# Output products moved inside the rounds of half-size products, one more at a chunk's head, no round in the chunk of the last values, and another buffer in the tail

## The chip, the cores and the metric

One core of one Trainium2 chip. The metric is the device time of one execution in microseconds (us). The kernel before takes 332.12 us (median of 3 runs, 332.07 to 332.22). "Span" is what the profiler sees of an execution, from its first to its last instruction or transfer; the time was 1.7 to 3.6 us longer than the span in these runs.

## The reference, cut to what matters

Pooled attention, then a gated two-layer block. Batch 8, 8 heads, 576 rows, head size 64; 4608 tokens of 512 values, inner size 1536.

```python
def _attn_ref(q, k, v):                      # k and v are averaged over 8 rows first
    scores = scale * np.matmul(q, k_p.transpose(0, 1, 3, 2))
    attn = np.exp(scores - scores.max(-1, keepdims=True))
    return np.matmul(attn / attn.sum(-1, keepdims=True), v_p)

def _moe_ref(x, w_gate, w_val, w_out):
    return (np.maximum(x @ w_gate, 0.0) * (x @ w_val)) @ w_out
```

## The kernel before

The tokens are taken in nine chunks of 512 (0 to 8). In each chunk TensorE makes twelve **units** (`gate_val`: eight matmuls of 512 columns, giving one block of 128 rows of `h`), and beside them the output products of the chunk before and the attention of the batch that a later chunk needs. Attention ends in chunk 6: its scores and **values** are woven between the units there, and VectorE has the values to scale.

From chunk 1 on, the output layer uses a scheme with seven half-size products for eight (Strassen's, in Winograd's form). From the end of chunk 6 on, the first layer does so too: a **hidden product** makes two blocks of `h` (fo and fo + 6), which would take two units, with seven half-size products (pr1 to pr7, four matmuls of 256 columns each: 28 in place of the 32 that two units come to). Two of them, x and y, are interleaved into a **round**, with sums of x quarters or of `h` on VectorE between (`s`), and two output products P (twelve matmuls of 256 columns). A **bank** is the tile in TensorE's accumulation memory that a product is written to; before another product may overwrite it, ScalarE has to copy it out or VectorE to add it to something (a **take**).

```python
def hidden_products(c, fo, z):
    ...
    def pr1():
        bank("a")
        product("a", plain(0, fs), e, True)
        nc.scalar.copy(p1, ps["a"])            # ScalarE empties bank a for pr6
    def pr2():
        bank("b", ps_at, "at")
        product("b", plain(1, fs), g, True)
        take("b", p1, fo, lo)()                # take: VectorE adds, GpSimd finishes h
    def pr5():
        bank("c")
        product("c", summed(0), T[0], True)
        nc.scalar.copy(p5, ps["c"])            # ... bank c for pr3
    def pr6():
        product("a", summed(1), T[1], False)
        nc.scalar.copy(u2, ps["a"])            # ... bank a for pr7
    def pr3():
        product("c", summed(3), h, False)
    def pr7():
        product("a", summed(2), T[2], False)
        ends.append(take("a", p5, n_hf + fo, hi, nc.scalar))   # VectorE empties bank a for pr4
    def later():                               # x[9], y[9]
        ends.append(take("c", u2, fo, hi, nc.scalar))
    def pr4():
        product("a", plain(1, fu), T[3], False)
        ...                                    # relu on ScalarE, product on VectorE

def hidden_round(c, fo, others, sums):
    x, y = [hidden_products(c, fo + z, z) for z in range(2)]
    first, second = others
    s = sums
    return [x[1], s[0], x[2], s[1], y[1], y[2], s[2], x[5], s[3], x[6], *first,
            y[5], x[3], x[7], x[9], y[6], y[3], x[4], x[8], y[7], *second, y[9], y[4], y[8]]

def out_products(c, last=False):               # one accumulation bank for all seven
    rows = [half_pool.tile([P, 2, DM], F32, name=f"rows{i}", bufs=2 - i) for i in range(2)]
    ...
    order = [pr1, pr2, pr6, pr7, pr5, pr3, pr4] if last else \
        [pr1, pr2, pr6, pr7, pr4, pr5, pr3]
```

In the text below, "x4" is pr4 of x. Chunk 6 ran eight units and one round, chunk 7 three rounds, chunk 8 two rounds and four units, then a tail that makes chunk 8's own output.

The softmax here doesn't subtract the row's maximum and nothing guards it: scores larger than these inputs give would overflow.

## Time and profile before

| | before |
|---|---|
| time | 332.12 us |
| span of the profiled run | 330.3 us |
| TensorE busy | 96% of the span |
| VectorE busy | 68% |
| rounds of half-size products | 6 (chunk 6 one, chunk 7 three, chunk 8 two) |
| gaps in TensorE's matmul stream from 220 us on, of more than 0.1 us | 9, together 3.86 us |

A matmul's row shows a duration of 0.27 us for 256 columns, but these overlap, so the distance between starts is what counts. A gap is the start of a group less the start of the group before and that group's matmuls times 0.109 us (256 columns) or 0.216 (512). Nine gaps: six before x4 (2.27 us), two before an output product that follows another (1.02), one in the tail (0.57).

### The profile page before, as it was taken

To read this page: it belongs to the slowest core of one execution; us is meant where nothing else is said; L and a number is where in the kernel's file an instruction comes from. 1 tells how busy PE (TensorE), PEld (TensorE's weight loads), DVE (VectorE), ACT (ScalarE), POOL (GpSimd) and SP (SyncE) were. 2 spreads that over 40 slices of the span, in tenths; PEclk is the share of its full clock that TensorE was granted. 3 is DMA by queue.
4 is the path that set the end of the run, shared out by engine and by line. 5 is a ranking of instruction groups with operands and counts; after the bars stand their busy time and mean duration, and the time that the engine had idled before them with its cause. 6 is when DMAs were issued, how large, how long until landed. Compare 5 with 4: busy or idle time off the path is not lost.

```text
span 330.3 us, 7017 instructions
## 1 busy us (share of the span) xinstructions
PE 318.4 (96%) x2670; PEld 226.7 (69%) x2670; DVE 225.7 (68%) x482; ACT 152.1 (46%) x353; POOL 207.0 (63%) x258
## 2 busy tenths in 40 slices
PE   7899999999999999999999999999999999999994
PEld 2577885555566656666989866656668888888673
DVE  7455637667675856696569544974699988878761
ACT  1444482374555227522762266126715665565230
POOL 8557608999999924963399029999604676567100
PEclk9999999999999999999999999999999999999998
DMA  7999998997859439999893480332021310120134
GB/s 110 187 202 202 200 214 146 192 166 143 166 101 176 90 90 107 55 168 179 127 186 65 101 122 0 51 73 82 0 42 33 87 41 2 33 98 3 25 108 123
DMA packets 51011, 35.46 MB, mean 107 GB/s; under 512 B 30433, under 2 KB 45025, under 8 KB 50977
## 3 DMA queue, kind: packets, MB, share of 16 engines
q0 software_dynamic: 18304, 18.88, 36.4%
q1 hardware_dynamic: 32528, 16.00, 26.1%
q8 instruction: 21, 0.34, 0.4%
q10 hardware_dynamic: 144, 0.13, 0.1%
q14 instruction: 14, 0.11, 0.1%
HBM read 37.75 MB, written 9.44 MB: 143 GB/s over the span
## 4 chain that ended last, share of the span: by engine, by line
PE 81%; DVE 11%; DMA 4%; issue 1%; POOL 1%; SPq 1%; ACT 0%; DVEq 0%; POOLq 0%
PE mm_ps L430 42%; PE acc_ps L523 17%; PE mm_ps L743 6%; PE at_ps L311 4%; PE mm_ps L468 3%; PE at_ps L389 3%; DVE sum L514 3%; DVE px L759 2%; DMA out_dram<-rows 2%; DMA q<-in_q_dram 2%; PE at_ps L743 1%; DVE px L395 1%; DVE rows L531 1%; DVE h L439 1%; DVE sum L594 1%
## 5 line engine op out<-in xcount | busy, mean ns | idle before, releaser
L439 DVE TENSOR_TENSOR h<-mm_ps,relu 128x512 f16<-128x512 f32 (+1 forms) x96 | 59.8, 624 | 69.5 <-PE mm_ps L430 60.1
L436 ACT ACTIVATE relu<-mm_ps 128x512 f16<-128x512 f32 (+1 forms) x96 | 52.2, 544 | 101.8 <-PE mm_ps L430 96.4
L430 PE MATMUL mm_ps<-x_T,wg_sb 128*128 128x512 f16 (+1 forms) x432 | 88.5, 331 | 0.0
L430 PE MATMUL mm_ps<-x_T,wv_sb 128*128 128x512 f16 (+1 forms) x432 | 88.4, 332 | 0.0
L430 PEld LDWEIGHTS <-wv_sb 128*128 128x128 f16 x432 | 42.2, 98 | 30.5 <-DVE kpT0u L264 0.2
L430 PEld LDWEIGHTS <-wg_sb 128*128 128x128 f16 x432 | 38.9, 98 | 19.5
L325 ACT ACTIVATE expT<-at_ps 72x288 f16<-72x288 f32 (+2 forms) x128 | 38.9, 375 | 13.7 <-PE at_ps L311 13.6
L523 PEld LDWEIGHTS <-sum 128*128 128x128 f16 x336 | 32.0, 98 | 7.0 <-issue 1.3
L395 DVE TENSOR_TENSOR px<-at_ps,prd 128x256 f16<-128x256 f32 (+1 forms) x80 | 33.8, 423 | 2.7
L181 POOL TENSOR_TENSOR tree_b<-tree_a 72x256 f32<-72x256 f32 (+1 forms) x42 | 33.5, 799 | 3.3
L765 POOL TENSOR_TENSOR h<-px 128x256 f16<-128x256 f16 x36 | 25.4, 718 | 13.7 <-ACT px L762 12.7
L523 PE MATMUL acc_ps<-wo_sums,sum 128*128 128x256 f16 x252 | 30.9, 272 | 0.3 <-DVE mid L531 0.3
L175 POOL TENSOR_TENSOR tree_a<-k_in 96x512 f32<-96x512 f16 x18 | 21.5, 1197 | 14.4 <-DMA k_in<-in_k_dram 14.4
L175 POOL TENSOR_TENSOR tree_a<-v_in 72x512 f32<-72x512 f16 x24 | 28.7, 1197 | 0.1
L523 PEld LDWEIGHTS <-h 128*128 128x128 f16 x252 | 23.7, 98 | 2.8
L764 POOL TENSOR_SCALAR px<-px 128x256 f16<-128x256 f16 x12 | 13.1, 1092 | 18.9 <-DVE px L759 18.9
L843 POOL COPY gate<-h 128x1 f16<-128x1 f16 x4 | 1.5, 381 | 33.7 <-DVE h L439 33.7
L523 PE MATMUL acc_ps<-wo_sb,h 128*128 128x256 f16 x168 | 20.6, 272 | 0.0
L514 DVE TENSOR_TENSOR sum<-h 128x768 f16<-128x768 f16 x28 | 18.8, 670 | 0.0
L531 DVE TENSOR_TENSOR rows<-acc_ps,mid 128x512 f32<-128x512 f32 x21 | 14.4, 686 | 4.9 <-PE acc_ps L523 4.8
L389 PEld LDWEIGHTS <-expT 72*128 72x128 f16 (+1 forms) x280 | 12.9, 100 | 5.9 <-DVE prd L394 0.8
L394 DVE RECIPROCAL prd<-at_ps 128x4 f32<-128x4 f32 (+1 forms) x80 | 13.7, 171 | 3.7 <-PE at_ps L389 3.6
(144 smaller groups left out, 526.0 us busy)
## 6 DMA issues: line engine op xcount, KB each, us to landing
out_dram<-rows SPq DMA_DIRECT2D x24, 256.0 KB
k_in<-in_k_dram POOLq DMA_DIRECT2D x7, 576.0 KB, 8.2
q<-in_q_dram POOLq DMA_DIRECT2D x7, 576.0 KB, 11.6
v_in<-in_v_dram POOLq DMA_DIRECT2D x6, 576.0 KB, 14.4
wg_sb<-in_moe_w_gate_dram POOLq DMA_DIRECT2D x6, 256.0 KB, 11.6
wv_sb<-in_moe_w_val_dram POOLq DMA_DIRECT2D x6, 256.0 KB, 11.4
wo_sb<-in_moe_w_out_dram POOLq DMA_DIRECT2D x3, 512.0 KB, 9.6
v_in<-in_v_dram POOLq DMA_DIRECT2D x2, 512.0 KB, 11.6
```

Source lines behind the costliest of these rows:

```text
L175: eng.tensor_tensor(out=cell["a"][:n], in0=src[:, :, :4 * D], in1=src[:, :, 4 * D:], op=ALU.add)
L181: eng.tensor_tensor(out=cell["c"][:n], in0=a[:n, :, :2 * D], in1=a[:n, :, 2 * D:], op=ALU.add)
L325: nc.scalar.activation(out=out_ap, in_=in_ap, func=AF.Exp, scale=EXP_SCALE)
L389: nc.tensor.matmul(out=ps[:n, c0:c0 + D + 1], lhsT=weights(b, h, t), rhs=stats[b % 2][:SP, g, s0:s0 + D + 1], start=True, stop=True,)
L395: nc.vector.tensor_tensor(out=x[:n, half * NG // 2:(half + 1) * NG // 2, :, :], in0=pv.rearrange("p g (x c) -> p g x c", x=2)[:, :, :, :D] ...
L430: nc.tensor.matmul(out=t[:, lo:hi], lhsT=w[:, ci, fsl], rhs=x_T[:, ci, x0:x0 + hi - lo], start=(ci == 0), stop=(ci == n_co - 1),)
L436: nc.scalar.activation(out=relu[:, :n], in_=ps[0][:, :n], func=AF.Relu)
L439: nc.vector.tensor_tensor(out=h_tiles[c][:, fo, t0:t0 + n], in0=ps[1][:, :n], in1=relu[:, :n], op=ALU.mult)
L514: nc.vector.tensor_tensor(out=S[k][:, i], in0=x[:, i], in1=y[:, i], op=op)
L523: nc.tensor.matmul(out=ps[:, tb, :], lhsT=lhs[:, i, tb * P:(tb + 1) * P], rhs=rhs[:, i, :], start=(first and tb == 0 and i == 0), stop=(tb ...
L743: nc.tensor.matmul(out=ps[key][:, m], lhsT=w_of(m)[:, i], rhs=xs[:, i], start=(first and m == 0 and i == 0), stop=(m == 1 and i == N_CO - ...
L765: nc.gpsimd.tensor_tensor(out=hc[:, fo_out, cols], in0=gv[:, 0], in1=gv[:, 1], op=ALU.mult)
```

## The change

The intent: fill the places where TensorE waits for other engines with output products, and have no round in chunk 6, where VectorE also has the values to do. Four edits, cut to the core:

```diff
@@ tail: its second output tile
-            rows.extend(half_pool.tile([P, 2, DM], F32, name=f"rows{i}", bufs=2 - i)
-                        for i in range(2))
+            rows.extend(half_pool.tile([P, 2, DM], F32, name="rows0", bufs=2) for _ in range(2))
@@ hidden_round
-        first, second = others
-        return [x[1], s[0], x[2], s[1], y[1], y[2], s[2], x[5], s[3], x[6], *first,
-                y[5], x[3], x[7], x[9], y[6], y[3], x[4], x[8], y[7], *second, y[9], y[4], y[8]]
+        first, (second, third) = others[:-2], others[-2:]
+        return [x[1], s[0], x[2], s[1], y[1], y[2], *first, s[2], x[5], s[3], x[6],
+                y[5], x[3], x[7], x[9], y[6], second, y[3], x[4], x[8], y[7], third,
+                y[9], y[4], y[8]]
@@ attention: scores one unit later in chunk 6
-        return [[kt]] + [[]] * (b + 1 < B) + trios + [[p] for p in V], []
+        return [[kt], []] + trios + [[p] for p in V], []
@@ chunks 7 and 8: three products in a chunk's first round, none left over behind the last
-                    units += hidden_round(c, fo, ([prods.pop(0)], [prods.pop(0)]), mine)
+                    n = 2 if fo else 3
+                    units += hidden_round(c, fo, prods[:n], mine)
+                    del prods[:n]
@@ chunk 6: twelve units, no round; the x sums for chunk 7 at unit place 15
-                    order = [fo for fo in range(n_fo) if fo % n_hf > 1]
-                run(hidden_round(c, 0, (prods[:1], prods[1:]), sums[6:] + more[:2]) + more[2:])
+                elif c == C_HIDDEN - 1 and i == 15:
+                    run(x_sums_of(c + 1))
```

More of the change, by code (lines that the diff above doesn't have):

```diff
@@ L1010 @@
                 units = []
-                order = range(n_fo - 1)
-                if c == C_HIDDEN - 1:
-                    order = [fo for fo in range(n_fo) if fo % n_hf > 1]
-                for fo in order:
-                    if c == C_HIDDEN - 1 and len(prods) == 2:
-                        units.append(gv[fo])
-                        continue
+                for fo in range(n_fo - 1):
                     units.append(gv[fo])
@@ L1024 @@
                 prods, sums = out_products(c - 1, last)
+                if c == C_HIDDEN:
+                    take_mids()
                 units = []
@@ L1041, in begin_tail @@
                         run(ready[0])
-                    units += [prods.pop(0), gv[n_hf - 2], prods.pop(0), begin_tail,
+                    units += [gv[n_hf - 2], prods.pop(0), begin_tail,
                               gv[n_fo - 2], lambda: run(last_sums[1]), prods.pop(0),
@@ L1046 @@
                 else:
-                    units += prods
                     gv[-1] = lambda: None
@@ L1077 @@
                     hidden_weight_sums()
-                elif c == C_HIDDEN - 1 and i == 11:
-                    run(x_sums_of(c))
-            if c == C_HIDDEN - 1:
-                take_mids()
-                more = x_sums_of(c + 1)
-                run(hidden_round(c, 0, (prods[:1], prods[1:]), sums[6:] + more[:2]) + more[2:])
-            else:
-                gv[-1]()
+                elif c == C_HIDDEN - 1 and i == 15:
+                    run(x_sums_of(c + 1))
+            gv[-1]()
         run(last_sums[2])
```

## The prediction

> **What bounds the kernel now.** I read, in this order, the page's busy shares and the chain that ended last, the list of who waited for whom on TensorE, then the timelines of TensorE, VectorE and ScalarE over 215 to 330 us, where every changed line runs.
>
> ```profile
> PE 318.4 (96%) x2670; PEld 226.7 (69%) x2670; DVE 225.7 (68%) x482; ACT 152.1 (46%) x353; POOL 207.0 (63%) x258
> ...
> PE 81%; DVE 11%; DMA 4%; issue 1%; POOL 1%; SPq 1%; ACT 0%; DVEq 0%; POOLq 0%
> ```
>
> TensorE is busy 96% and makes up 81% of the chain: the kernel is a stream of matmuls, and only three things move its end: matmul columns, gaps in the stream, and the tail. VectorE's 11% of the chain marks where gaps come from.
>
> ```profile
> PE mm_ps L743 <- DVE px L759: 1.1, 2, 0.7
> PE mm_ps L602 <- DVE rows L608: 0.4, 1, 0.4
> PE acc_ps L523 <- DVE rows L531: 0.3, 1, 0.3
> PE acc_ps L523 <- DVE mid L531: 0.3, 1, 0.3
> ```
>
> Columns: total us, times, longest. These are TensorE's waits inside the changed stretches. The view counts only idle time after the modelled end of the pipelined matmul, so I measure gaps in starts instead.
>
> ```profile
> 246.58 1.03 PE L430 MATMUL mm_ps<-x_T,wg_sb 128*128 128x512 f16 x4
> 247.44 1.03 PE L430 MATMUL mm_ps<-x_T,wv_sb 128*128 128x512 f16 x4
> 248.30 0.38 PE L743 MATMUL mm_ps<-x_T,wg_sb 128*128 128x256 f16 x2
> ...
> 263.27 0.38 PE L743 MATMUL mm_ps<-x_T,v_in 128*128 128x256 f16 x2
> 263.49 0.38 PE L743 MATMUL mm_ps<-x_T,q 128*128 128x256 f16 x2
> 264.57 0.38 PE L743 MATMUL mm_ps<-expT,wg_sb 128*128 128x256 f16 x2 [0.70 <-DVE px L759]
> ...
> 284.87 0.38 PE L743 MATMUL mm_ps<-expT,wv_sb 128*128 128x256 f16 x2
> 285.60 1.47 PE L523 MATMUL acc_ps<-wo_sb,sum 128*128 128x256 f16 x12 [0.34 <-DVE rows L531]
> ```
>
> Eight full-size matmuls (one gate/value unit) take 248.30 - 246.58 = 1.72 us of starts; two half-size ones 263.49 - 263.27 = 0.22. So a half-size product (four matmuls) costs 0.4375 us, an output product (twelve) 1.31. The pair at 263.49 should be followed at 263.71; x4 starts at 264.57, a gap of 0.86.
>
> ```profile
> 262.43 1.49 DVE L514 TENSOR_TENSOR sum<-sum,h 128x768 f16<-128x768 f16 x2
> 263.84 0.68 DVE L759 TENSOR_TENSOR px<-mm_ps,fout 128x512 f16<-128x512 f32 x1
> 264.44 0.68 DVE L759 TENSOR_TENSOR px<-mm_ps,qT 128x512 f16<-128x512 f32 x1
> ```
>
> That is why: product 4 of x writes the bank that product 7 of x just filled, once VectorE has taken it (start 263.84). VectorE was still in sums.
>
> A round is two hidden products, x and y, of seven half-size products each, plus two output products P: x1 x2 y1 y2 x5 x6 P y5 x3 x7 y6 y3 x4 y7 P y4. The same subtraction, start of x4 minus the end of y3, gives 0.55, 0.86, 0.27, 0.17, 0.14 and 0.28 us in the six rounds (chunk 6 one, chunk 7 three, chunk 8 two): 2.27. After chunk 7's and after chunk 8's last round, the leftover P directly follows another P in the single accumulation bank save for y4: 0.51 us each (285.09 to 285.60; 304.79 to 305.30). Together 3.29 us, about 1% of the time.
>
> **What the Trainium skill says.** "TensorE: Matmul & The Clock Gate", section "Back-to-back issue gap", lists 262 cycles for 256 columns and 518 for 512 at 2.4 GHz, so 109 and 216 ns. The trace agrees: 109.4 and 216, at a granted clock of 1.00 in these stretches. The same section gives 131 ns for 512 columns in a sustained stream; this trace doesn't show that. So weight loads hide even behind half-size matmuls, and seven products for eight is a true saving. "SBUF — State Buffer", section "Who interferes with whom", says that a VectorE instruction with two SBUF inputs and a GpSimd instruction that reads SBUF contend, and the second to issue blocks; the trace has sums of one shape that take from 0.54 to 1.5 us, the long ones while GpSimd works. "Perfetto Trace Analysis", section "Optimization Strategy", says that the same gap repeated on the engine that should be saturated can mean too few buffers; here it is the bank reuse above.
>
> **The change part by part.**
>
> 1. *No round in chunk 6.* The order listing shows TensorE 24 matmuls shorter: 56 half-size ones become 32 full-size ones. 14 x 0.4375 = 6.13 us becomes 4 x 1.73 = 6.92: **+0.80** on the path. The round's gap goes: **-0.55**. In the new order of chunk 6 one unit stands between the key transposes and the first scores; before, scores began 0.1 late there (227.26 to about 227.4): **-0.1**. I see no new wait: sum 1 for its product is issued no later, the last sum comes when GpSimd is idle (its weight sums end at 236.3), and x sums wait for a transposed piece sent some 10 us earlier.
>
> 2. *P moved from after x6 to after y6.* Between the end of x7 and x4 stood y6 and y3, 0.875 us, for VectorE's 0.6 us take plus about 0.25 from product end to start. Now there are 2.19 us. The other gaps of chunks 7 and 8 are 0.86 + 0.27 + 0.17 + 0.14 + 0.28 = 1.72: **-1.72**. But x3 now starts only 0.875 after x5 and x7 0.875 after u2's product x6, and both overwrite a bank that ScalarE copies out first:
>
> ```profile
> 269.63 0.59 ACT L783 COPY fout<-mm_ps 128x512 f32<-128x512 f32 x1 [0.23 <-PE mm_ps L743]
> 270.11 0.59 ACT L787 COPY qT<-mm_ps 128x512 f32<-128x512 f32 x1
> ```
>
> Here x5 ended at 269.37, so its copy ends 0.85 after it, plus about 0.05 for the signal (the leftover P started 0.05 after VectorE's end at 285.55): 0.90 against 0.875. The second copy ends 270.70, 0.89 after x6's end at 269.81. So about 0.03 and 0.06 us of new wait. VectorE follows: its sums end 5.06 us into that round (272.25 against 267.19), takes run to 5.7 and 6.3, the add that evacuates P to 6.9 or 7.1. x4 would start at 6.13, fine; the second P, which needs that add, would at 7.0: 0 to 0.2 us lost. I put **+0.15 per round in the three rounds with two P**, and nearly nothing in the two head rounds, where the extra P gives 1.31 us more: +0.5.
>
> 3. *A third P at the head of a chunk's first round.* No leftover P remains behind another: **-1.02**. The count of P stays; the head P finds its bank long free.
>
> 4. *The tail's second output tile is a buffer of rows0.* Before, it was rows1, whose store was still in flight:
>
> ```profile
> 324.08 1.09 DVE L608 TENSOR_TENSOR rows<-mm_ps,mid 128x256 f32<-128x256 f32 x3 [2.02 <-DMA out_dram<-rows]
> ```
>
> TensorE ran six matmuls from 323.33, should have gone on at 323.98, and did at 324.56: 0.58 lost. The store of the new buffer is issued some 5 us earlier, so I give **-0.55**; the last store follows the last matmul as before.
>
> Sum: 0.80 - 0.55 - 0.1 - 1.72 + 0.5 - 1.02 - 0.55 = **-2.6 us**: 332.1 becomes **329.5 us**.
>
> **Rivals.**
>
> *The wait only changes its name.* The copies of x5 and x6 (0.02 to 0.06 short), or VectorE's add behind the takes, cost 0.4 to 0.6 us in each of five rounds. For it: the margins above are tenths, and VectorE is busy some 8 of 9 us in a round. Against: ScalarE had caught up by x5 in each round of the trace, and VectorE loses chunk 6's leftover sums. It would give 331 us or more.
>
> *Chunk 6 pays more than columns.* Four more relu activations and score exponentials in ScalarE's queue, or late transposes, could stall TensorE there. Against: TensorE ran from 220 to 248 with hardly a gap. It would add 0.5 to 1.5: 330 to 331.
>
> *The tail gives nothing,* if the store queue rather than rows1 sets the end: 330.1. The 0.58 gap in TensorE speaks against it.
>
> *Better than that:* no new wait anywhere: 329.0.
>
> **Range and chances.** All gaps gone gives 329.0; one rival in full some 330 to 331. I say **328.8 to 330.8**, 8 times in 10. Even removing every gap saves 0.9%, and the worst rival only cancels it, so within 2% has 0.98, faster 0.01, slower 0.01.
>
> **What would show it.** In the changed profile: no gap over 0.2 before x4 in the rounds of chunks 7 and 8; x3 and x7 starting within 0.1 of the product before; no P behind a P; chunk 7's first round starting at about 257.7 (before, its first round started at 257.6); gate/value unit 4 of chunk 8 starting near 304.5 (before 306.6); no wait on a store in the tail, and the span down to about 327.7. The prediction is wrong if a new wait of half a microsecond recurs in each round, named after ScalarE's copies or VectorE's add, or if chunk 6 takes over 1 us more.

## The result, and the profile after

The changed kernel takes 329.95 us (median of six runs; 329.3 to 330.14 in the five fast ones, whose median is 329.85 and mean 329.82, and one slow run of 341.65, over 1.5% above the fastest, which is left out of the comparison), beside 332.17 us of the kernel before. The ratio of fast runs is 0.9927, with a 95% interval of 0.9912 to 0.9941. Ratios here are the mean of one kernel's fast runs over the mean of the other's of the same rounds, so not quite the ratio of the medians. By the 2% rule that is "same"; the interval excludes no change. 329.5 was predicted.

The page of the changed kernel, its busy shares and the chain that ended last:

```profile
PE 319.0 (97%) x2646; PEld 224.3 (68%) x2646; DVE 223.6 (68%) x474; ACT 148.7 (45%) x345; POOL 200.6 (61%) x250
...
PE 91%; DVE 4%; DMA 2%; ACT 1%; issue 1%; POOL 1%; DVEq 0%; ACTq 0%; POOLq 0%
```

TensorE went from 81% to 91% of the chain, VectorE from 11% to 4%, and the span from 330.3 to 327.8 us. Of the four waits in the prediction's list none is left; what the list of TensorE's waits still has in this stretch is one that was there before too, an output product of chunk 5:

```profile
PE acc_ps L523 <- DVE sum L514: 0.3, 1, 0.3
```

TensorE in a round with two output products (chunk 7's second), timeline of the changed kernel; `expT,wg_sb` is x4, `x_T,v_in` opens x3 at 271.38 and y3 at 274.05, and `expT,v_in` at 271.87 is x7:

```profile
271.38 0.38 PE L742 MATMUL mm_ps<-x_T,v_in 128*128 128x256 f16 x2
271.59 0.38 PE L742 MATMUL mm_ps<-x_T,q 128*128 128x256 f16 x2
271.87 0.38 PE L742 MATMUL mm_ps<-expT,v_in 128*128 128x256 f16 x2
...
274.05 0.38 PE L742 MATMUL mm_ps<-x_T,v_in 128*128 128x256 f16 x2
274.26 0.38 PE L742 MATMUL mm_ps<-x_T,q 128*128 128x256 f16 x2
274.48 0.38 PE L742 MATMUL mm_ps<-expT,wg_sb 128*128 128x256 f16 x2
```

x4 follows y3 without a gap (274.26 + 0.22 = 274.48); x7 starts 0.06 late (271.59 + 0.22 = 271.81). ScalarE says why:

```profile
270.74 0.59 ACT L782 COPY fout<-mm_ps 128x512 f32<-128x512 f32 x1
271.22 0.59 ACT L786 COPY qT<-mm_ps 128x512 f32<-128x512 f32 x1
```

The second copy, of x6's bank, ends at 271.81, and x7 starts 0.06 later. The tail, on VectorE: the adds no longer stand in a bunch behind a store.

```profile
319.94 0.42 DVE L608 TENSOR_TENSOR rows<-mm_ps,mid 128x256 f32<-128x256 f32 x1 [2.17 <-PE mm_ps L602]
320.53 0.42 DVE L608 TENSOR_TENSOR rows<-mm_ps,mid 128x256 f32<-128x256 f32 x1 [0.16 <-PE mm_ps L602]
321.91 0.42 DVE L608 TENSOR_TENSOR rows<-mm_ps,mid 128x256 f32<-128x256 f32 x1 [0.95 <-PE mm_ps L602]
```

The first 220 us differ by up to 1.7 us between traces of kernels that are the same there (unit 10 of chunk 5 began at 220.16 to 221.85 us in before, changed, after_again and e1 to e6). So I compare distances inside a trace, from the start of that unit (0.0), which is ahead of all that the change moves on TensorE:

| from unit 10 of chunk 5 to | before | changed | e1 tail | e2 move | e3 move undone | e4 round kept | e5 no head |
|---|---|---|---|---|---|---|---|
| the first half-size product (of chunk 6's round or, without it, chunk 7's first) | 27.83 | 37.23 | 27.84 | 27.84 | 37.23 | 27.84 | 37.22 |
| unit 4 of chunk 8 | 86.13 | 83.96 | 86.13 | 85.26 | 85.03 | 83.63 | 84.81 |
| end of span | 109.83 | 106.85 | 108.97 | 108.96 | 107.94 | 106.58 | 107.65 |
| unit 4 to end of span | 23.70 | 22.89 | 22.84 | 23.70 | 22.91 | 22.95 | 22.84 |

The changed kernel gains 2.17 us up to unit 4 of chunk 8 and 0.81 in the tail, 2.98 in all. The spans are read to 0.1 us, so the last two rows hold to 0.05.

### The profile page after: what moved, and what is told of

Its sections match the earlier page's. It is cut to its first block, busy times and chain, and to the rows that moved or that the text cites. A ratio compares the mean times of both kernels' runs of the same rounds, so it can differ in the third digit from the quotient of the medians.

```text
span 327.8 us, 6935 instructions
## 1 busy us (share of the span) xinstructions
PE 319.0 (97%) x2646; PEld 224.3 (68%) x2646; DVE 223.6 (68%) x474; ACT 148.7 (45%) x345; POOL 200.6 (61%) x250
## 4 chain that ended last, share of the span: by engine, by line
PE 91%; DVE 4%; DMA 2%; ACT 1%; issue 1%; POOL 1%; DVEq 0%; ACTq 0%; POOLq 0%
PE mm_ps L430 44%; PE acc_ps L523 19%; PE mm_ps L742 8%; PE at_ps L311 4%; PE mm_ps L468 3%; PE at_ps L389 3%; PE mm_ps L602 2%; DMA q<-in_q_dram 2%; PE at_ps L742 1%; DVE px L395 1%; DVE h L439 1%; PE mm_ps L412 1%; DVE sum L514 1%; PE mm_ps L282 1%; PE mm_ps L342 1%
## 5 line engine op out<-in xcount | busy, mean ns | idle before, releaser
L439 DVE TENSOR_TENSOR h<-mm_ps,relu 128x512 f16<-128x512 f32 (+1 forms) x100 | 62.6, 626 | 71.8 <-PE mm_ps L430 62.4
L436 ACT ACTIVATE relu<-mm_ps 128x512 f16<-128x512 f32 (+1 forms) x100 | 54.6, 546 | 106.5 <-PE mm_ps L430 101.1
L430 PE MATMUL mm_ps<-x_T,wv_sb 128*128 128x512 f16 (+1 forms) x448 | 92.6, 333 | 0.4 <-DVE kpT0u L264 0.4
L430 PE MATMUL mm_ps<-x_T,wg_sb 128*128 128x512 f16 (+1 forms) x448 | 92.6, 333 | 0.0
L430 PEld LDWEIGHTS <-wv_sb 128*128 128x128 f16 x448 | 43.7, 98 | 33.1 <-DVE kpT0u L264 0.9
L430 PEld LDWEIGHTS <-wg_sb 128*128 128x128 f16 x448 | 40.5, 98 | 20.9 <-issue 0.3
L764 POOL TENSOR_TENSOR h<-px 128x256 f16<-128x256 f16 x30 | 21.3, 724 | 13.6 <-ACT px L761 12.8
L763 POOL TENSOR_SCALAR px<-px 128x256 f16<-128x256 f16 x10 | 10.9, 1087 | 24.8 <-DVE px L758 24.8
L514 DVE TENSOR_TENSOR sum<-h 128x768 f16<-128x768 f16 x28 | 19.9, 712 | 0.0
```

What stands on the lines that cost most here:

```text
L430: nc.tensor.matmul(out=t[:, lo:hi], lhsT=w[:, ci, fsl], rhs=x_T[:, ci, x0:x0 + hi - lo], start=(ci == 0), stop=(ci == n_co - 1),)
L436: nc.scalar.activation(out=relu[:, :n], in_=ps[0][:, :n], func=AF.Relu)
L439: nc.vector.tensor_tensor(out=h_tiles[c][:, fo, t0:t0 + n], in0=ps[1][:, :n], in1=relu[:, :n], op=ALU.mult)
L514: nc.vector.tensor_tensor(out=S[k][:, i], in0=x[:, i], in1=y[:, i], op=op)
L764: nc.gpsimd.tensor_tensor(out=hc[:, fo_out, cols], in0=gv[:, 0], in1=gv[:, 1], op=ALU.mult)
```

## The experiments

All results were correct. My theory: each of the gaps has the cause that the prediction names, so each edit by itself gives back its own gaps. Rivals: the move of P only renames the wait; dropping chunk 6's round is what removes VectorE's lateness; the tail gains nothing. Ten runs follow, nine new kernels and the changed one again, five rounds each, in three sets that each share runs of the kernel before. The numbers in us up to unit 4 are from one trace each.

### e2: only the move

```diff
 # on the kernel before
-  ... s[3], x[6], *first, y[5], x[3], x[7], x[9], y[6], y[3], x[4], ...
+  ... s[3], x[6], y[5], x[3], x[7], x[9], y[6], *first, y[3], x[4], ...
```

> The kernel before with one edit: in every round the first output product stands after y6 instead of after x6; nothing else. My theory: the gaps before x4 of the six rounds (2.27 us in all) fall to under 0.1 each, x3 and x7 get waits of 0.02 to 0.06, the second P perhaps 0.1 to 0.2; the two leftover gaps of 0.51 and the tail's 0.58 stay. So 1.6 to 2.0 us less than before, about 330.4. Rival (the wait only changes its name, to ScalarE's copies or VectorE's add): within 0.6 of before, with gaps of 0.3 or more before x3, x7 or the second P in each round.

Measured: 331.31 us beside 332.2; ratio 0.9983 (0.9955 to 1.0012), so not told from no change by time. In the trace, 0.87 us less up to unit 4. Five of six gaps before x4 are gone, and x7 waits 0.05, as expected. But in chunk 7's first round the gap of 0.86 is still 0.79, with an output product now standing in it, and chunk 6's round has a new one of 0.26 before its second P. TensorE, then VectorE, of this kernel:

```profile
263.24 0.38 PE L743 MATMUL mm_ps<-x_T,q 128*128 128x256 f16 x2
264.25 0.38 PE L743 MATMUL mm_ps<-expT,wg_sb 128*128 128x256 f16 x2 [0.63 <-DVE px L759]
```

```profile
258.58 0.66 DVE L710 TENSOR_TENSOR expT<-x_T 128x512 f16<-128x512 f16 x1
259.17 0.88 DVE L710 TENSOR_TENSOR expT<-x_T,expT 128x512 f16<-128x512 f16 x1
...
261.51 0.68 DVE L759 TENSOR_TENSOR px<-at_ps,qT 128x512 f16<-128x512 f32 x1
262.11 1.49 DVE L514 TENSOR_TENSOR sum<-sum,h 128x768 f16<-128x768 f16 x2
263.52 0.68 DVE L759 TENSOR_TENSOR px<-mm_ps,fout 128x512 f16<-128x512 f32 x1
```

VectorE is without a pause from the x sums that chunk 6's round left (L710, 1.40 us: 258.58 to 259.98) to the take at 263.52 that frees x4's bank. The product put before x4 gave TensorE nothing: the take starts at 263.52, in the kernel before at 263.84. A product put ahead of the wait hardly helps where the engine waited for is late with its whole queue. My expectation of 1.6 to 2.0 was wrong here; of the 3.29 us of gaps up to unit 4, 2.33 stay, new ones counted; in chunk 6's round the rival was half right, since there the wait of 0.55 became one of 0.26 at VectorE's add.

### e3: the changed kernel with the move undone

```diff
 # on the changed kernel
-  ... x[6], y[5], x[3], x[7], x[9], y[6], second, y[3], x[4], ...
+  ... x[6], second, y[5], x[3], x[7], x[9], y[6], y[3], x[4], ...
```

> The changed kernel with that one part undone: the second output product back after x6. My theory: a gap of 0.15 to 0.3 comes back before x4 in each of the five rounds, the 0.02 to 0.06 before x3 and x7 go: 0.6 to 1.1 us more than the changed kernel. Less than e2 gains, since the two large gaps of before (0.55 and 0.86) also had VectorE's leftover sums of chunk 6 in them. Rival (the move is worth nothing once the sums are gone): within 0.2 of the changed kernel. Rival (VectorE is late whatever the order): gaps of 0.5 and more return, 2 us more.

Measured: 331.04 us; ratio to before 0.9971. In the trace 1.07 us more than the changed kernel up to unit 4. The gaps before x4 come back at 0.13 to 0.18, 0.79 together, as the theory says, and the 0.05 before x7 go. There are two more that I had not expected, 0.32 and 0.39, inside the first P of the second rounds of chunks 7 and 8. TensorE and VectorE in chunk 7, one timeline:

```profile
270.29 0.49 PE L523 MATMUL acc_ps<-wo_sums,sum 128*128 128x256 f16 x3
270.33 0.55 DVE L514 TENSOR_TENSOR sum<-h 128x768 f16<-128x768 f16 x1
...
270.94 1.16 PE L523 MATMUL acc_ps<-wo_sums,sum 128*128 128x256 f16 x9 [0.17 <-DVE sum L514]
```

With three products in the first round, the product that is now first in the second round needs a sum made in that same round; its second half is done at 270.88. So the head product and the later place belong together: the head makes each later product due one place earlier.

### e5: the changed kernel without the head product

```diff
 # on the changed kernel
-                    n = 2 if fo else 3
+                    n = 2
@@ chunk 8, and the like in chunk 7
-                    units += [gv[n_hf - 2], prods.pop(0), begin_tail,
+                    units += [prods.pop(0), gv[n_hf - 2], prods.pop(0), begin_tail,
```

> The changed kernel without the product at the head: two output products in each round, one left over behind each chunk's rounds as before. My theory: two gaps of 0.51 before the leftover products come back and nothing else: 0.9 to 1.1 us more than the changed kernel. Rival (the head product costs as much in VectorE or ScalarE waits as the leftover did): within 0.3 of the changed kernel.

Measured: 331.0 us; ratio to before 0.9954. In the trace 0.85 us more than the changed kernel up to unit 4: both gaps of 0.51 return, some of the small ones go. Close to what was expected (0.9 to 1.1). One thing more: the 0.86 before x4 of chunk 7's first round does not return. VectorE, then TensorE, of this kernel, whose round began at 259.07:

```profile
263.50 0.68 DVE L758 TENSOR_TENSOR px<-mm_ps,fout 128x512 f16<-128x512 f32 x1
```

```profile
264.98 0.38 PE L742 MATMUL mm_ps<-x_T,q 128*128 128x256 f16 x2
265.20 0.38 PE L742 MATMUL mm_ps<-expT,wg_sb 128*128 128x256 f16 x2
```

The take that frees x4's bank starts 4.43 us into the round; in e2, whose round began at 257.28, it is 6.24. This kernel has no head product, but no round in chunk 6 either. With e4 below, which has a head product and chunk 6's round, the gap is gone too. So that gap needs chunk 6's round **and** a first round without a head product; taking away either is enough. That it is the round's x sums that make VectorE late is read from e2's trace (1.40 of the 1.81 us between 4.43 and 6.24); no run took away these sums alone.

### e4: the changed kernel with chunk 6's round kept

```diff
 # on the changed kernel: chunk 6 as in the kernel before
+                    order = [fo for fo in range(n_fo) if fo % n_hf > 1]
-                    run(x_sums_of(c + 1))
+                run(hidden_round(c, 0, prods, sums[6:] + more[:2]) + more[2:])
```

> The changed kernel with chunk 6 as before: eight full units and one round, with its x sums, and scores one unit earlier. My theory: the round saves its 0.80 us of columns and has no gap over 0.1, the key transposes cost 0.1: about 0.6 us less than the changed kernel, 329.3, faster than both. Rival (dropping the round was needed: the sums it leaves to VectorE make waits of 0.3 to 0.9 in it and in chunk 7's first round): no gain or up to 0.5 more than the changed kernel, with gaps before x4 or the second P there.

Measured: 328.68 us; ratio to before 0.9897 (0.9879 to 0.9915). In the trace 0.33 us less than the changed kernel up to unit 4. The 0.80 us of columns is saved, but the round has a gap of 0.26 before its second P, the scores of chunk 6 begin 0.1 late as in the kernel before, and one of 0.09 comes in chunk 7. So about half of the 0.6 us expected. VectorE of this kernel:

```profile
253.50 0.77 DVE L709 TENSOR_TENSOR expT<-x_T,expT 128x512 f16<-128x512 f16 x1
254.20 0.68 DVE L758 TENSOR_TENSOR px<-mm_ps,fout 128x512 f16<-128x512 f32 x1
254.80 0.68 DVE L758 TENSOR_TENSOR px<-mm_ps,qT 128x512 f16<-128x512 f32 x1
255.40 0.67 DVE L531 TENSOR_TENSOR rows<-acc_ps,mid 128x512 f32<-128x512 f32 x1
```

Its queue reaches the add that empties P's bank at 255.40, and P, ready at 255.86, starts at 256.12. So the rival is right that the round makes VectorE late, and wrong that dropping it was needed: with the head product in chunk 7 the round pays 0.33 us in the trace. The time differs by more: the mean of fast runs is 328.89 us for e4, 329.82 and 329.55 for the changed kernel in its two sets (e4 ran in another set than either; the common measure is the kernel before, and the intervals of the ratios overlap). But the spans of the same runs are 327.10, 327.46 and 327.42 on average. Some 0.35 us is thus the kernel's; the rest of the difference lies outside the span, and its cause is open (e8).

### e1: only the tail

```diff
 # on the kernel before: the tail's edit of the change, nothing else
```

> The kernel before with one edit: the tail's second output tile is a buffer of rows0. My theory (VectorE waited for the store of rows1, TensorE for VectorE, 0.57 us): no gap before the last twelve matmuls, and from the start of unit 4 of chunk 8 to the end of the span 23.7 us becomes 22.9 (the changed kernel has 22.9), all else as before: 0.6 to 0.8 us less than before. Rival (the last store follows the store queue, not TensorE): the gap goes, but the end stays within 0.2 of before.

Measured: 331.4 us beside 332.57; ratio 0.9969 (0.9948 to 0.9989). From unit 4 to the end 22.84 us instead of 23.70, and the same 86.13 before it. TensorE of this kernel goes on without a gap (324.49 + 0.65 = 325.14):

```profile
324.49 0.82 PE L602 MATMUL mm_ps<-wo_sums,sum 128*128 128x256 f16 x6
325.14 1.49 PE L602 MATMUL mm_ps<-wo_sums,h 128*128 128x256 f16 x12
```

The gain is 0.86, of which TensorE's gap is 0.57. The rest, a quarter of a microsecond, lies behind TensorE: from the start of the last twelve matmuls to the end of the span it is 5.74 us before (330.3 - 324.56) and 5.46 here (330.6 - 325.14). Before, the four last stores of the sync queue were issued in one go, 324.53 to 327.02, so 2.46 us past the start of the last twelve matmuls; here they are spread from 323.88 to 327.04, 1.90 past it. That the end follows this queue is likely, but not shown: no run changed the stores alone.

### after_again: the changed kernel once more, beside the next two

> The changed kernel itself, unedited, to stand beside the two next on one chip: 0.7 per cent less than before, 2.2 to 2.6 us, gaps as in its first trace.

Measured: 329.34 us (328.75 to 330.97), ratio 0.9911 (0.9885 to 0.9938); 83.95 us up to unit 4. The gaps repeat to 0.01 us.

### e6: e4 with the x sums behind the round

```diff
 # on e4
-                run(hidden_round(c, 0, prods, sums[6:] + more[:2]) + more[2:])
+                run(hidden_round(c, 0, prods, sums[6:] + [lambda: None] * 2) + more)
```

> The kernel with the round of chunk 6 kept (e4), and one edit: the first two x sums for chunk 7 leave that round's middle and stand with the other two behind the round. My theory (e4's gap of 0.26 before that round's second output product is VectorE's queue: two sums, two takes, then the add): that gap falls under 0.05, chunk 7's first round hides the four sums behind its head product: 0.2 to 0.4 less than e4, 1.0 to 1.4 less than the changed kernel. Rival (VectorE's queue only moves on): a gap of 0.2 to 0.9 before x5 or x4 of chunk 7's first round, no gain.

Measured: 328.64 us, ratio 0.9888. The 0.26 is gone, and 0.15 comes before x4 of chunk 7's first round: 0.11 us less than e4 in the trace up to unit 4, less than expected. Most of VectorE's lateness only moved on.

### e7: e4 with a pause in GpSimd's weight sums

One gap of 0.43 is in every kernel so far: three matmuls into an output product of chunk 5, TensorE waits for a sum of VectorE. GpSimd sums weights beside it. The edit makes GpSimd copy a column of `h` that unit 9 of chunk 5 makes, so its sums pause until that is there.

```diff
 # on e4
         for f0 in range(0, F_HALF, 2 * P):
+            if f0 == 2 * P:
+                nc.gpsimd.tensor_copy(out=gate, in_=h_tiles[C_HIDDEN - 2][:, n_fo - 3, :1])
```

> The kernel with the round of chunk 6 kept (e4), and one edit: GpSimd's weight sums stop after their first eight until VectorE has made h of unit 9 of chunk 5. My theory (VectorE's last sums of chunk 5 take 0.9 to 1.4 us instead of 0.55 because GpSimd's adds run beside them, and so an output product waits 0.43 inside): the sums take about 0.55 and that gap goes, GpSimd ends its sums some 3.5 us later, before they are read: 0.3 to 0.5 less than e4. Rival (those sums are late for another reason, the data or the queue): the gap stays at 0.3 or more and the time is e4's.

Measured: 328.62 us (327.85 to 329.66), ratio 0.9885 (0.9862 to 0.9909). The gap is gone. The two sums on VectorE, in the kernel before and then in this one:

```profile
216.55 1.44 DVE L514 TENSOR_TENSOR sum<-h,sum 128x768 f16<-128x768 f16 x1
...
218.51 0.91 DVE L514 TENSOR_TENSOR sum<-h,sum 128x768 f16<-128x768 f16 x1
```

```profile
216.19 0.55 DVE L514 TENSOR_TENSOR sum<-h,sum 128x768 f16<-128x768 f16 x1
...
217.44 0.55 DVE L514 TENSOR_TENSOR sum<-h,sum 128x768 f16<-128x768 f16 x1
```

GpSimd in this kernel is still for 3.28 us, from 216.1 on:

```profile
219.38 0.19 POOL L689 COPY gate<-h 128x1 f16<-128x1 f16 x1 [3.28 <-DVE h L439]
```

The same two instructions take 0.55 us each when GpSimd is still, and 1.44 and 0.91 beside its adds. That shows the cause of the gap. In time it can't be told from e4.

### e9: e6 and e7 together

> The kernel with the round of chunk 6 kept (e4), with the late x sums of e6 and the gate of e7 together. Theory (their gaps are in different places and add up): from unit 10 of chunk 5 to unit 4 of chunk 8 83.5 us as in e6, no gap of 0.43 ahead of it as in e7; 0.5 less than e4, about 328.3, 1.2 per cent under the kernel before. Rival (GpSimd's later sums slow VectorE's x sums and the gain of one is lost): 83.8 or more in that stretch, time of e7.

Measured: 328.64 us (four runs, 328.47 to 329.25), ratio 0.9892. The trace shows what the theory said: 83.52 us up to unit 4, and no 0.43 ahead of it. The time shows nothing of it: e4, e6, e7 and e9 all have medians of 328.6 to 328.7. Differences of 0.1 to 0.4 us are below what five rounds tell apart here, and I don't claim a gain of e9 in time.

### e8: what stays outside the span

The changed kernel, e3 and e5, which have no round in chunk 6, took 1.95 to 3.63 us over their span in their 23 fast runs; before, e1, e2, e4, e6, e7 and e9, which have it, about 1.7 to 1.9.

```diff
 # on the changed kernel, in chunk 2: eight small copies each on VectorE, GpSimd and ScalarE
+                    for eng, pad in zip((nc.vector, nc.gpsimd), pads):
+                        for x in range(8):
+                            eng.tensor_copy(out=pad[:, x:x + 1], in_=ident16[:, x:x + 1])
+                    for x in range(8):
+                        nc.scalar.copy(pads[2][:, x:x + 1], ident16[:, x:x + 1])
```

> The changed kernel and, in chunk 2, eight more copies of one column on each of VectorE, GpSimd and ScalarE, written to tiles that nobody reads; they bring the three engines to the instruction counts of the kernel before. It asks why the time of the changed kernel is 2.0 to 2.9 us over its span, where the kernel before and all with chunk 6's round are 1.7 to 1.9 over theirs. Theory (the length of those engines' programs): 1.7 to 1.9 over the span, so about 0.4 less time at the same span or 0.1 to 0.3 more. Rival (TensorE's program, or the order of instructions, or nothing of the kind): still 2.0 to 2.9 over the span.

Measured: 331.4 us, ratio 0.9994; over the span 1.76, 1.82, 1.88, 1.89, 2.36 and 2.72. Four of six runs are in the lower band, where no run of the changed kernel was, but the spans themselves grew (328.6 to 332.2). That is inconclusive. The length of the programs may have to do with it; nothing here settles it.

## Why the prediction was right, and where not

The time was inside the range, 0.45 us above the point by the median of all runs and 0.35 by that of the fast ones. The sum of the steps nearly holds in the trace, though one step got its gain from another part of the change, and that the time came so near the point is partly luck (last point). Point by point:

- **Chunk 6** (+0.80, -0.55, -0.1; net +0.15). From unit 10 of chunk 5 to the first round of chunk 7 it is 37.23 us after against 37.12 before (257.59 - 220.47): **+0.11**. Right; the columns are counted, +0.80, and the round's gap (0.55) and the late scores (0.1) are gone. No rival of chunk 6 came about.
- **The move** (-1.72, +0.5 of new waits). In the changed kernel all gaps before x4 are gone, as predicted, but the step is mis-assigned. It said that each gap is closed because 0.875 us become 2.19. For 0.86 of the 1.72 that is wrong: e2 has the 2.19 us and a gap of 0.79. That gap was VectorE's queue, filled by chunk 6's x sums, and it goes with chunk 6's round or with the head product (e5, e4); e3, without the move, has 0.13 left there. Alone, the move is worth 0.87, chunk 6's round included; undone, it costs 1.07, since the head product makes it needed (e3).
- **New waits** (+0.15 in three rounds, nearly nothing in head rounds). Measured: about 0.02 before x3 in four of the five rounds, 0.05 to 0.06 before x7 in all five, 0.08 before the last P of chunk 8: 0.44 together. The sum was right partly by luck: the three rounds with two P have 0.31 where 0.45 was forecast (VectorE's add held up only one second P), the two head rounds 0.13 where nearly nothing was. They have the waits too; in the changed timeline of chunk 7's, ScalarE's copies follow one another from 261.44 on, the first being that of the head product. The 0.02 and 0.06 themselves came out as worked from the copies' ends.
- **The head** (-1.02). Right: e5 brings both gaps of 0.51 back, and loses 0.85 net of small waits that go.
- **The tail** (-0.55). Measured **-0.81** in the changed kernel and -0.86 by itself. The cause was right; "the last store follows the last matmul as before" was not: the end came a quarter of a microsecond nearer to the last matmul, with the stores issued earlier (e1).
- **The sum.** The trace gains 2.98 us, the prediction said 2.6, and the time gains 2.2 by the medians, 2.4 by the means of fast runs. Two misses offset each other: the trace gained 0.4 more than predicted, mostly in the tail, and the time is 2.0 to 2.8 over the span, where before it was 1.7 to 1.9, which the prediction did not foresee; why is open (e8). The profiled span, 327.8, is close to the predicted 327.7 by luck too: this trace reached unit 10 of chunk 5 0.49 us later than the one before did (220.95 against 220.47).

The mean over fast runs says the same: spans of 327.46 us, times of 329.82, 2.36 over. The kernel before has spans of 330.6 and times of 332.4 on average, in the 32 fast runs beside the experiments.

## What to carry to other kernels

Where an engine waits for another, ask whether that other is late with one instruction or with its queue: work put in front of the wait covered the first here (gaps of 0.14 to 0.28), and took 0.07 of 0.86 off the second. Take each part of a change apart before crediting it: the head product and the dropped round each close a gap that the move was credited with, the move closes gaps that the head product opens, and keeping the round (e4) was 0.33 us better in the trace than dropping it. When the expected gain is below 1%, read it from distances within traces, since the same stretch at the start of these kernels took times up to 1.7 us apart.

## What the Trainium skill lacked or had wrong

- "TensorE: Matmul & The Clock Gate", section "Back-to-back issue gap", gives 131 ns for 512 columns as the sustained spacing in a stream of weight loads and matmuls and calls 216 ns the isolated one. In this stream of pairs the spacing was 216 ns (eight matmuls in 1.72 us) and 109 ns for 256 columns, at a granted clock of 1.00: its isolated formula holds here.
- "Perfetto Trace Analysis", section "Summary: the profiler window per engine type", says that semaphore propagation is hidden from the profile, and that page gives no size. In these runs ScalarE's copy began 0.26 us after the modelled end of issue of the product it waited for (269.37 to 269.63), and TensorE went on about 0.05 us after an add or a copy of VectorE or ScalarE had ended (285.55 to 285.60; 271.81 to 271.87).
- "SBUF — State Buffer", section "Who interferes with whom", is right that VectorE's instructions with two SBUF inputs and GpSimd's block each other, and gives no size for such sums: those of 0.55 us took 0.91 and 1.44 beside GpSimd's adds (e7), and GpSimd's adds, in the kernel before, 1.35 and 1.47 in place of 1.15.
- No page tells why a time can be 1.7 us over the span in one kernel and 2.0 to 3.6 in another of fewer instructions.
